# A gated state-space convolution on one core: seeds written to PSUM by ScalarE, a second table stored slot by slot, and the log step as one row

## The chip, the cores and the metric

The kernel runs on one core of a Trainium2 chip. The metric is the device time in microseconds (us); the median of three runs of the kernel before is 164.76 us (164.47 to 164.81). Engines are named as the profile names them: PE (matmuls; PEld is its weight load), DVE (VectorE), ACT (ScalarE), POOL (GpSimd), SP (the queue that issues most DMAs). Each engine takes its instructions strictly in the order of its own list, and engines wait for each other by semaphores.

## The reference

`x` is 2048 tokens of 512 channels in bf16. The output is `g*a + (1-g)*b`. `g` is a sigmoid of a dot product per token. `b` is `x`, with a small gated network added at the two tokens that rank highest. `a` is a state-space convolution:

```python
dt = jnp.exp(log_dt)[:, None]
logdA = dt * A                       # A complex, 512 channels x 128 states
dB = dt * Bc
P = jnp.exp(logdA[:, :, None] * l)   # l = 0..2047
K = jnp.einsum("dn,dnl,dn->dl", Cc, P, dB).real
# y = causal convolution of u with K along the tokens, by FFT, plus u * Dskip
```

## The kernel before, in words

**Two halves.** The 512 channels are worked in two halves `h` of 256, the 2048 tokens in two blocks `blk` of 1024.

**Tables.** A power `exp(logdA * l)` is split into a product of two tables, because a lag `l` is written as a sum of a coarse and a fine lag. `tab1(h)` makes table 1 (`TP[h]`), with 32 coarse lags. `tab2(h)` makes table 2: the magnitudes `EB` come from ACT's Exp (`exps2`), the angles pass through `trig` (a scaling into int32, `L455`; a Sin on ACT; a quarter-turn addition, `L611`; a second Sin), and DVE multiplies them (helper `TT`, `L436`). From 11 magnitudes and angles DVE builds the four weighted tables `r[0]` to `r[3]` with 21, 17, 21 and 17 slots. In memory a group of 4 channels keeps all its slots together, so the innermost run of an operand is 4 elements times the slots. The weights `WW` are `C * B * dt`, made at the start by `PBR`, `CM1`, `CM2`, `CMW` and a last multiply by `DTB = exp(log_dt)`; `log_dt` is loaded as a 128-fold broadcast.

**Kernel spectrum.** `kgen(h)` multiplies table 1 with table 2 on PE (`L819`, 256 matmuls of 84 or 68 columns per half) and ACT copies the sums to `KA`. Three small sets of matmuls (`L832`, `L836`, `L845`, `L848`) pick the entries into `KC`. `kspec(h)` turns `KC` into the spectrum `KK[h]` for two segments `i` (`L865`). For `i = 1` the sum carries over the other part of segment 0 with alternating sign, by two 512-column matmuls with a diagonal of plus and minus one (`kc`, `L872`). Each of the 16 pieces of `KK` over both halves is copied from PSUM by ACT (`L451`).

**Input spectrum, products and inverse.** `forward(blk)` (`L801`) makes the input's spectrum `X`. `products(h)` is DVE alone (`L436`): per half eight multiplies or adds of 4096 elements and some sixteen of 1024 elements. `inverse(h)` accumulates in PSUM, for 16 token blocks per half: `fin` starts a bank with `DG * U` (`L919`: the input, scaled by a diagonal that holds `(1-g)/g` per token) and `OHR * ZB` (`L920`: rows for single tokens), then the inverse transform is added (`L933`), and a copy scaled by `g` writes the result (`L941`), which a DMA stores.

**What sets the order.** The program lists 627 operations. `ORDER` is a string of their numbers, three characters each, that fixes the order on every engine. Many copies and scalings have two forms, one for ACT and one for DVE: the string `SECOND` chooses, one digit per operation (helpers `EV`, `SCL` and the quarter-turn addition). `PLACES` gives each temporary its PSUM bank (eight of them) or buffer place; an operation that takes a place waits for all uses of the holder before. No engine can pass over an operation that waits.

Of the kernel before, what the change touches and what calls it, by code (L numbers as in the profile page):

```python
# [337 lines left out]
def small_mats():  # L338
    eye = np.eye(128)
    sgn = np.diag(np.where(np.arange(128) % 2 == 0, 1.0, -1.0))  # L340
# [17 lines left out]
    "02z04j06305n04v04k04l01n01e03603704m06403803003903103a01304105103b01l02503201202401r03c03d05a05902703u02200b03e04w03g03h05q05205r03f02a03i01802301t04n"
    "04z02003j05o03k06601p05s03l04203m05c03n02900m05002b01y03o03p04o03q05t02802605306504x03r06705b04y05w03s05u05d05605405505p05705x05e05g05y07d05803z06l07f"
    "04005f07e07g06x05h07h06z07i04804506y03v03w05z05v07005i07j04307107807607507707906007207306807a07b08y08x03t06m09603x08z04604407404909907c06103y01404a07l"  # L360
    "08w07n09709807k09004706g09a06f07m07p07o06a07z07s04b04c07y06907q07v07w04d04e07t09106h06i06n09207u06p09b07r07x06o08008209s06s09r08109t09309406b09q06j06k"
# [659 lines left out]
```

## Time and profile before

| what | value |
|---|---|
| median of three runs | 164.76 us |
| profiled execution, its own time | 164.17 us |
| its span in the trace | 162.3 us, so 1.87 us lie around the span |
| PE busy | 141.7 us, 87% of the span |
| DVE busy | 151.5 us, 93% |
| ACT busy | 120.0 us, 74% |
| granted TensorE clock, mean | 0.989 |
| DMA moved | 18.00 MB |

How to read it: busy time counts an instruction from its start to its end. Two instructions that follow each other on one engine without a wait overlap a little, so what one more instruction costs is read from start to start. Most DVE work has one helper line, `L436`, so its shapes have to be kept apart.

### The profile page before, as it was taken

What the parts mean: (1) busy time and instruction counts of PE and PEld (TensorE: products, weight loads), DVE (VectorE), ACT (ScalarE), POOL (GpSimd) and SP (SyncE); (2) the same over time, 40 slices, a digit from 0 to 9 for tenths busy, and PEclk for the clock granted to TensorE, in tenths of its full rate; (3) what the DMA queues carried; (4) which work ended last, traced back from release to release, by engine and by line L of the source; (5) the groups of instructions that cost most, each with busy time, mean ns of one, the idle gap of its engine ahead of it and who ended that gap; (6) DMA issues with size and microseconds to landing.
All of it is one profiled execution on the core that took longest, in us unless ns stands there. A gap on an engine that the chain in (4) does not pass through costs nothing.

```text
span 162.3 us, 3993 instructions
## 1 busy us (share of the span) xinstructions
PE 141.7 (87%) x1721; PEld 104.7 (65%) x1733; DVE 151.5 (93%) x234; ACT 120.0 (74%) x181; POOL 4.1 (3%) x10
## 2 busy tenths in 40 slices
PE   0579996869999999999777997999999999999990
PEld 0456642335763634686675867977888888788880
DVE  0499999999999999999999999999999999999982
ACT  3399999999999999999999595756783522260461
POOL 3000020000000000000000000040000000000000
PEclk9999999999999999999987999999999999999999
DMA  2999999900000000000790000007700020023036
GB/s 73 334 398 367 413 406 383 312 13 0 4 0 0 4 0 0 4 0 4 220 408 22 4 2 0 4 4 222 307 0 0 0 69 0 2 66 99 0 106 185
DMA packets 11251, 18.00 MB, mean 111 GB/s; under 512 B 857, under 2 KB 7898, under 8 KB 11106
## 3 DMA queue, kind: packets, MB, share of 16 engines
q1 hardware_dynamic: 10114, 16.97, 29.5%
q10 hardware_dynamic: 1120, 0.79, 1.7%
q8 instruction: 13, 0.21, 0.5%
q14 instruction: 4, 0.03, 0.1%
HBM read 15.66 MB, written 2.10 MB: 109 GB/s over the span
## 4 chain that ended last, share of the span: by engine, by line
DVE 48%; PE 10%; ACT 0%; issue 0%
DVE AR L436 43%; PE ps L933 9%; DVE AR L455 2%; DVE AR L611 1%; DVE AR L941 1%; PE ps L920 1%; PE ps L919 1%; ACT AR L941 0%; DVE AR L445 0%
## 5 line engine op out<-in xcount | busy, mean ns | idle before, releaser
L436 DVE TENSOR_TENSOR AR<-AR 128x1024 bf16<-128x1024 bf16 (+8 forms) x121 | 114.1, 997 | 0.4
L451 ACT ACTIVATE AR<-ps 128x1024 bf16<-128x1024 f32 (+5 forms) x48 | 42.6, 930 | 14.1 <-PE ps L865 4.0
L447 ACT ACTIVATE AR<-AR 128x512 bf16<-128x512 f32 (+4 forms) x73 | 50.5, 753 | 2.8 <-DVE AR L436 1.8
L801 PE MATMUL ps<-AR 128*128 128x512 bf16 x183 | 41.8, 379 | 1.4 <-DVE AR L445 0.4
L801 PEld LDWEIGHTS ps<-AR 128*128 128x128 bf16 x192 | 18.0, 98 | 21.0 <-DVE AR L445 0.9
L933 PE MATMUL ps<-AR 128*128 128x256 bf16 x256 | 30.6, 273 | 0.2 <-DVE AR L436 0.2
L933 PEld LDWEIGHTS ps<-AR 128*128 128x128 bf16 x256 | 24.8, 98 | 4.1 <-DVE AR L436 1.0
L941 ACT ACTIVATE AR<-ps,AR 128x256 bf16<-128x256 f32 x27 | 11.9, 473 | 19.3 <-PE ps L933 19.0
L819 PEld LDWEIGHTS ps<-AR 128*128 128x128 bf16 x512 | 18.1, 97 | 3.3 <-ACT AR L451 2.0
L819 PE MATMUL ps<-AR 128*128 128x84 bf16 (+1 forms) x512 | 18.6, 197 | 1.5 <-DVE AR L436 0.9
L865 PE MATMUL ps<-AR 128*128 128x256 bf16 x160 | 19.0, 275 | 0.9 <-ACT AR L451 0.9
L865 PEld LDWEIGHTS ps<-AR 128*128 128x128 bf16 x160 | 15.3, 99 | 4.6 <-ACT AR L451 2.0
L455 DVE TENSOR_SCALAR AR<-AR 128x256 int32<-128x256 f32 (+2 forms) x41 | 12.6, 328 | 0.1
L455 ACT ACTIVATE AR<-AR 128x256 int32<-128x256 f32 (+1 forms) x25 | 11.2, 482 | 0.0
L557 PE MATMUL ps<-AR 128*128 128x128 bf16 x24 | 3.1, 308 | 5.7 <-DMA AR<-c_bf 5.7
L920 PE MATMUL ps<-AR 128*128 128x256 bf16 x32 | 7.8, 273 | 0.0
L919 PE MATMUL ps<-AR 128*128 128x256 bf16 x32 | 7.8, 272 | 0.0
L611 DVE TENSOR_SCALAR AR<-AR 128x1024 int32<-128x1024 int32 x10 | 6.9, 687 | 0.1
L436 DVE TENSOR_TENSOR AR<-AR,ps 128x512 f32<-128x512 bf16 x1 | 0.7, 689 | 6.5 <-PE ps L557 6.5
L557 PEld LDWEIGHTS ps<-AR 128*128 128x128 bf16 x24 | 2.3, 139 | 6.0 <-DMA AR<-c_bf 5.7
L670 PE MATMUL ps<-AR 128*128 128x128 bf16 x64 | 4.7, 222 | 1.1 <-DMA AR<-in_A_u_dram 0.7
L832 PE MATMUL ps<-AR 128*32 128x128 bf16 x64 | 5.0, 422 | 0.4 <-ACT AR L451 0.4
(57 smaller groups left out, 88.3 us busy)
## 6 DMA issues: line engine op xcount, KB each, us to landing
AR<-c_ksp SPq DMA_DIRECT2D x5, 512.0 KB, 5.6
AR<-in_A_u_dram SPq DMA_DIRECT2D x4, 512.0 KB, 6.2
AR<-c_fwd SPq DMA_DIRECT2D x4, 512.0 KB, 12.1
AR<-c_inv SPq DMA_DIRECT2D x1, 2048.0 KB, 7.8
AR<-in_B_w_up_dram SPq DMA_DIRECT2D x1, 1792.0 KB, 14.7
AR<-in_B_w_gate_dram SPq DMA_DIRECT2D x1, 1792.0 KB, 18.2
out_dram<-AR SPq DMA_DIRECT2D x14, 128.0 KB, 2.2
AR<-in_B_w_down_dram SPq DMA_DIRECT2D x1, 1024.0 KB, 13.7
```

Of the source, the lines that this page charges most:

```text
L436: return P.op(DVE, lambda h: h.tensor_tensor(out=o, in0=a, in1=b, op=op), rd, wr, cost=tt_cost(o, a, b), **k)
L447: return P.op(ACT, lambda h: h.activation(out=o, in_=a, func=func, scale=scale, bias=bias), rd, wr, cost=0.185 + nel(o) * 0.833e-3 + (0.09 ...
L451: return P.op((ACT, DVE), (lambda h: h.activation(out=o, in_=a, func=ACTF.Copy), lambda h: h.tensor_copy(o, a)), rd, wr, cost=(0.185 + n * ...
L455: return P.op((ACT, DVE), (lambda h: h.activation(out=o, in_=a, func=ACTF.Copy, scale=c), lambda h: h.tensor_scalar(out=o, in0=a, scalar1= ...
L611: P.op((DVE, ACT), (lambda hh: hh.tensor_scalar(out=w, in0=w, scalar1=16384.0, scalar2=None, op0=ALU.add), lambda hh: hh.activation(out=w, ...
L801: last = h.matmul(o, w, x, start=(pm + par + st == 0), stop=(par == 1 and st == 3), skip_group_check=(pm == 1))
L819: last = hh.matmul(pb(0, 128, g // 6 * 512 + g % 6 * W4 + o, (1, n)), TP[h][1 - i // 2](0, 128, (b0 + g) * 128, (1, 128)), r[i](0, 128, (b ...
L865: last = hh.matmul(pb(0, 128, n * 256, (1, 256)), KP[u](0, 128, tau * 128, (1, 128)), KC[h](0, 128, jg * 256, (1, 256)), start=(k == 0 and ...
L919: hh.matmul(pb(0, 128, e * 256, (1, 256)), DG(0, 128, tb[e] * 128, (1, 128)), U(0, 128, tb[e] * D + h * HC, (1, HC)), start=(e == 0), stop ...
L920: last = hh.matmul(pb(0, 128, e * 256, (1, 256)), OHR(0, 128, tb[e] * 128, (1, 128)), ZB(0, 128, h * HC, (1, HC)), start=False, stop=False)
L933: r = hh.matmul(pb(0, 128, e * 256, (1, 256)), G(0, 128, ((par * 2 + part) * 4 + ft) * 512 + (2 * t2 + e) * 128, (1, 128)), X(0, 128, h * ...
L941: P.op((ACT, DVE), (lambda hh, o=o, i_=i_, g_=g_: hh.activation(out=o, in_=i_, func=ACTF.Copy, scale=g_), lambda hh, o=o, i_=i_, g_=g_: hh ...
```

## The change

**Seeds.** In `kspec`, for `i = 1`, ACT copies the carry from `KK` straight into the PSUM banks, scaled by a sign per partition (`SGN`, a new 1 KB load), and the matmuls add to it; the 16 matmuls `kc` go. In `inverse`, ACT writes `U * (1-g)/g` into each half bank (32 copies of 256 elements) and only the `OHR * ZB` matmul of `fin` remains; the 32 matmuls on `DG`, `DG` itself (one DVE multiply of 2048 elements) and its small copy in `SGB` go. A seeded bank has to follow a holder that matmuls wrote in full.

**Table 2.** `EB`, `DI`, `QA`, `NB` and `r` are stored slot by slot: 256 channels of a slot lie together. Multiplies that differ only in an operand's offset become one instruction. `kgen` now reads its columns from `r` in runs of 4 elements, 512 bytes apart.

**Log step and weights.** `log_dt` is loaded as one row of 1 KB; a matmul with a row of ones spreads it over the partitions in PSUM, and Exp reads it there. `dt` is multiplied into `B` (`BDT`, in place of the copy `PBR`), so that the last multiply into `WW` goes.

**Order.** `ORDER`, `SECOND` and `PLACES` are replaced whole (644 operations). At the start SP now issues the row, the identity (`c_bf`) and `A_im`, ACT issues `A_re`. The copy `XE` may run on either engine. Costs noted for the ordering (`STT`) change without effect on the program.

```diff
-    sgn = np.diag(np.where(np.arange(128) % 2 == 0, 1.0, -1.0))
...
-    return np.concatenate([eye, sgn, -sgn, xs.reshape(128, -1), ek.reshape(128, -1)], 1), oh
...
-        DQ([(LDT(0, 128, 0, (1, D)), dr(A_log_dt, 0, (0, 128), (1, D)))], [], [LDT], 131072, eng=ACT)
-        prm_l(0)
         DQ([(CB(0, 128, 0, (1, 128)), cb_c[:, 0:128])], [], [(CB, "i")], 32768)
-        prm_l(1, eng=ACT)
+        prm_l(0, eng=ACT)
+        DQ([(LDT(0, 1, 0, (1, D)), dr(A_log_dt, 0, (D, 1), (1, D)))], [], [LDT], 1024)
+        prm_l(1)
+        P.op(POOL, lambda h: h.memset(ONE(0, 1, 0, (1, 128)), 1.0), [], [ONE], cost=0.2)
...
+        DQ([(SGN(0, 128, 0, (1, 2)), sg_c[:, :])], [], [SGN], 1024)
...
-        AC(f512(DTB), f512(LDT), ACTF.Exp, [LDT], [DTB], tset=0)
+        ld = misc()
+        P.op(PE, lambda h: h.matmul(ld(0, 128, 0, (1, D)), ONE(0, 1, 0, (1, 128)), LDT(0, 1, 0, (1, D)), start=True, stop=True), [LDT, ONE], [ld], cost=0.22)
+        AC(f512(DTB), ld(0, 128, 0, (1, D)), ACTF.Exp, [ld], [DTB], tset=0)
...
-        P.op((ACT, DVE), (lambda h: h.activation(out=w4(PBR, 0, (D, 2)), in_=pp(3, 0, (D, 2)), func=ACTF.Copy), lambda h: h.tensor_copy(w4(PBR, 0, (D, 2)), pp(3, 0, (D, 2)))), [pps[3]], [PBR], cost=(1.04, 1.23))
-        TT(w4(CM1, 0, (D, 2)), pp(2, 0, (D, 2)), w4(PBR, 0, (0, 2)), ALU.mult, [pps[2].buf, PBR], [CM1])
-        TT(w4(CM2, 0, (D, 2)), pp(2, 0, (D, 2)), w4(PBR, D, (0, 2)), ALU.mult, [pps[2].buf, PBR], [CM2])
-        TT(f512(CMW), f512(CM1), f512(CM2, D), ALU.subtract, [CM1, CM2], [(CMW, 0)])
-        TT(f512(CMW, D), f512(CM1, D), f512(CM2), ALU.add, [CM1, CM2], [(CMW, 1)])
-        TT(c2(WW), c2(CMW), DTB(0, 128, 0, (0, 2), (1, D)), ALU.mult, [CMW, DTB], [WW])
+        TT(w4(BDT, 0, (D, 2)), pp(3, 0, (D, 2)), w4(DTB, 0, (0, 2)), ALU.mult, [pps[3], DTB], [BDT])
+        TT(w4(CM1, 0, (D, 2)), pp(2, 0, (D, 2)), w4(BDT, 0, (0, 2)), ALU.mult, [pps[2], BDT], [CM1])
+        TT(w4(CM2, 0, (D, 2)), pp(2, 0, (D, 2)), w4(BDT, D, (0, 2)), ALU.mult, [pps[2], BDT], [CM2])
+        TT(f512(WW), f512(CM1), f512(CM2, D), ALU.subtract, [CM1, CM2], [(WW, 0)])
+        TT(f512(WW, D), f512(CM1, D), f512(CM2), ALU.add, [CM1, CM2], [(WW, 1)])
...
-                    AC(two(EB[0], EB[1], i * 4, 4 * NM), AL(0, 128, 0, (HC, 2), (4, 64), (1, 4)), ACTF.Exp, [AL], [(EB[0], ("e", i)), (EB[1], ("e", i))], scale=float(m), tset=ts)
...
+                    AC(pair(EB[0](0, 128, i * HC, (1, HC)), EB[1](0, 128, i * HC, (1, HC))), AL(0, 128, 0, (HC, 2), (1, HC)), ACTF.Exp, [AL], [(EB[0], ("e", i)), (EB[1], ("e", i))], scale=float(m), tset=ts)
...
-                return s(0, 128, k * n, (4, na_), (4 * na_, 64), (1, 4))
+                return s(0, 128, k * n, (4, na_), (4 * na_, 64), (1, 4)) if wide else s(0, 128, k * n, (HC, na_), (4, 64), (1, 4))
...
-                v = lambda b: b(0, 128, 4 * a0, (EW_, 64), (1, 4 * na_))
-                sv = lambda k: s(0, 128, k * na_ * HC, (4 * na_, 64), (1, 4 * na_))
-                if h == 0:
-                    TT(pair(v(di), v(eb)), pair(v(eb), v(eb)), pair(sv(0), sv(2)), MUL, [(s, "s"), (s, "c")], ek + [(di, g)])
-                else:
-                    TT(v(di), v(eb), sv(0), MUL, ek + [(s, "s")], [(di, g)])
-                    TT(v(eb), v(eb), sv(2), MUL, [(s, "c")], ek)
+                v = lambda b: b(0, 128, a0 * HC, (1, na_ * HC))
+                sv = lambda k: s(0, 128, k * na_ * HC, (1, na_ * HC))
+                TT(pair(v(di), v(eb)), pair(v(eb), v(eb)), pair(sv(0), sv(2)), MUL, [(s, "s"), (s, "c")], ek + [(di, g)])
...
-            TT(q(0), ww(1), bo(di), MUL, [WW] + dk, [(qa, 0)])
-            TT(q(1), ww(1), bo(eb), MUL, [WW] + ebk, [(qa, 1)])
-            TT(w(0), ww(0), bo(eb), MUL, [WW] + ebk, [(r[0], "w")])
-            TT(w(2), ww(0), bo(di), MUL, [WW] + dk, [(r[2], "w")])
+            sl = lambda b, j, *d: b(0, 128, j * HC, *d, (1, HC))
+            ww = lambda p: WW(0, 128, p * D + h * HC, (0, NOF), (1, HC))
+            bo = lambda b: sl(b, NST, (HC, NOF))
+            q = lambda i: sl(qa, i * NOF, (HC, NOF))
+            w = lambda i: sl(r[i], 0, (HC, NOF))
+            TT(pair(q(0), q(1)), pair(ww(1), ww(1)), pair(bo(di), bo(eb)), MUL, [(WW, 1)] + dk + ebk, [(qa, 0), (qa, 1)])
+            TT(pair(w(0), w(2)), pair(ww(0), ww(0)), pair(bo(eb), bo(di)), MUL, [(WW, 0)] + ebk + dk, [(r[0], "w"), (r[2], "w")])
...
-                for k, (j, a0, n) in enumerate(RAWS):
-                    o = o0 + sum(x[2] for x in RAWS[:k])
-                    bw = 4 * NJ if b is not nb else 4 * NOF
-                    TT(r[i](0, 128, 4 * o, (4 * (NJ, NR)[i % 2], 64), (4, n), (1, 4)), a(0, 128, 4 * a0, (EW_, 64), (4, n), (1, 4)), b(0, 128, 4 * j, (bw, 64), (0, n), (1, 4)), MUL,
-                       (ebk if a is eb else dk) + [(b, ka)], [(r[i], k)])
+                (j, a0, n), (j1, _, _), (j2, a2, n2) = RAWS
+                ak = (ebk if a is eb else dk) + [(b, ka)]
+                TT(sl(r[i], o0, (n * HC, 2), (HC, n)), sl(a, a0, (0, 2), (HC, n)), sl(b, j, ((j1 - j) * HC, 2), (0, n)), MUL, ak, [(r[i], 0)])
+                TT(sl(r[i], o0 + 2 * n, (HC, n2)), sl(a, a2, (HC, n2)), sl(b, j2, (0, n2)), MUL, ak, [(r[i], 2)])
...
-            CP(SGB(0, 128, 64, (2, 16), (1, 2)), SG(0, 128, 96, (1, 16), (0, 2)), [(SG, "x")], [(SGB, "x")])
...
-            CP(XE(32, NE, 0, (1, D)), xe(32, NE, 0, (1, D)), [xe.buf], [XE])
+            EV(XE(32, NE, 0, (1, D)), xe(32, NE, 0, (1, D)), [xe.buf], [XE])
...
-            TT(DG(0, 128, 0, (128, 16), (2, 64), (1, 2)), IDN(0, (0, 16), (2, 64), (1, 2)), SGB(0, 128, 64, (2, 16), (0, 64), (1, 2)), MUL, [CBI, (SGB, "x")], [DG])
...
                                 last = hh.matmul(pb(0, 128, g // 6 * 512 + g % 6 * W4 + o, (1, n)), TP[h][1 - i // 2](0, 128, (b0 + g) * 128, (1, 128)),
-                                                 r[i](0, 128, (b0 + g) * n, (1, n)), start=(i == 0), stop=(i == 3))
+                                                 r[i](0, 128, (b0 + g) * 4, (HC, n // 4), (1, 4)), start=(i == 0), stop=(i == 3))
...
-                        pb = psum(2)
+                        pb = psum(2, full=True, seed=i == 1)
                         taus = [part * 8 + pm * 4 + 2 * qd + e for pm in range(2) for e in range(2)]
+                        if i:
+                            AC(pb(0, 128, 0, (1, 1024)), KK[h](0, 128, (1 - part) * 2048 + qd * 1024, (1, 1024)), ACTF.Copy, [SGN, (KK[h], (0, 1 - part, qd))], [pb], scale=SGN(0, 128, part, (1, 1)))
                         def ks(hh, taus=taus, uses=uses, pb=pb, i=i, part=part):
                             last = None
                             for n, tau in enumerate(taus):
                                 for k, u in enumerate(uses):
                                     jg = KUSE[u][1]
-                                    last = hh.matmul(pb(0, 128, n * 256, (1, 256)), KP[u](0, 128, tau * 128, (1, 128)), KC[h](0, 128, jg * 256, (1, 256)), start=(k == 0 and (i == 0 or n % 2 == 0)), stop=(k == len(uses) - 1 and i == 0))
+                                    last = hh.matmul(pb(0, 128, n * 256, (1, 256)), KP[u](0, 128, tau * 128, (1, 128)), KC[h](0, 128, jg * 256, (1, 256)), start=(k == 0 and i == 0 and n % 2 == 0), stop=(k == len(uses) - 1 and n % 2 == 1), skip_group_check=(i == 1))
                             return last
                         P.op(PE, ks, [KP[u] for u in uses] + [(KC[h], KUSE[u][1]) for u in uses], [pb.buf], cost=4 * len(uses) * 0.1095)
-                        if i:
-                            def kc(hh, pb=pb, part=part, qd=qd):
-                                last = None
-                                for pm in range(2):
-                                    last = hh.matmul(pb(0, 128, pm * 512, (1, 512)), CB(0, 128, 256 if part == 0 else 128, (1, 128)),
-                                                     KK[h](0, 128, (1 - part) * 2048 + qd * 1024 + pm * 512, (1, 512)), start=False, stop=True)
-                                return last
-                            P.op(PE, kc, [(CB, "o"), (KK[h], (0, 1 - part, qd))], [pb.buf], cost=2 * 0.2157)
...
-                        pb = bufs[t2, par] = misc()
+                        pb = bufs[t2, par] = psum(seed=True)
+                        for e, tb in enumerate(tbs(t2, par)):
+                            AC(pb(0, 128, e * 256, (1, 256)), U(0, 128, tb * D + h * HC, (1, HC)), ACTF.Copy, [(SG, "x"), (U, (tb, h))], [(pb, e)], scale=SG(0, 128, 96 + tb, (1, 1)))
                         def fin(hh, pb=pb, tb=tbs(t2, par)):
                             last = None
                             for e in range(2):
-                                hh.matmul(pb(0, 128, e * 256, (1, 256)), DG(0, 128, tb[e] * 128, (1, 128)), U(0, 128, tb[e] * D + h * HC, (1, HC)), start=(e == 0), stop=False)
-                                last = hh.matmul(pb(0, 128, e * 256, (1, 256)), OHR(0, 128, tb[e] * 128, (1, 128)), ZB(0, 128, h * HC, (1, HC)), start=False, stop=False)
+                                last = hh.matmul(pb(0, 128, e * 256, (1, 256)), OHR(0, 128, tb[e] * 128, (1, 128)), ZB(0, 128, h * HC, (1, HC)), start=False, stop=False, skip_group_check=True)
                             return last
-                        P.op(PE, fin, [DG, OHR, (ZB, "y"), (ZB, ("e", h)), (ZB, "d")] + [(U, (t, h)) for t in tbs(t2, par)], [pb.buf], cost=4 * 0.1092)
+                        P.op(PE, fin, [OHR, (ZB, "y"), (ZB, ("e", h)), (ZB, "d")], [pb], cost=2 * 0.1092)
```

More of the change, by code (lines that the diff above doesn't have):

```diff
@@ L55, with __init__ @@
 class Life:
-    def __init__(self, prog, pool, n, home, region, name):
+    def __init__(self, prog, pool, n, home, region, name, full=False, seed=False):
+        self.full, self.seed = full or seed, seed
         self.prog, self.pool, self.n, self.region, self.name = prog, pool, n, region, name
@@ L150, in fixed @@
             ls.sort(key=lambda l: min(at[i] for i in l.all))
+            assert not ls[0].seed
             for a, b in zip(ls, ls[1:]):
+                assert a.full or not b.seed, "a seeded bank follows one that was not written in full"
                 assert max(at[i] for i in a.all) < min(at[i] for i in b.all), "a place is held twice"
@@ L358 @@
[L358 to L361, printed above, removed]
@@ L390, in bass_gated_mix__ssm_conv_s4__moe_arch_mod__prompt_kernel @@
     oh_c = const(oh, "c_oh")
+    sg_c = nc.inline_tensor(np.stack([np.where(np.arange(128) % 2 == 0, -1.0, 1.0), np.where(np.arange(128) % 2 == 0, 1.0, -1.0)], 1).astype(np.float32), "c_sgn").ap()
     cf = np.zeros((128, 160), np.float32)
@@ L418, in bass_gated_mix__ssm_conv_s4__moe_arch_mod__prompt_kernel, with psum @@
         oEND = 190 * KB + NM * 512
-        def psum(n=1, dt=F32, name="ps"):
+        def psum(n=1, dt=F32, name="ps", full=False, seed=False):
             def home(u):
@@ L422, in home @@
                 return (a if dt == F32 else a.bitcast(dt)), (u % 2) * (2048 // (4 if dt == F32 else 2))
-            return Life(P, "ps", n, home, None, name)
+            return Life(P, "ps", n, home, None, name, full, seed)
         def npe(n):
@@ L442, in STT @@
         def STT(o, a, sc, b, op0, op1, rd, wr, **k):
-            return P.op(DVE, lambda h: h.scalar_tensor_tensor(out=o, in0=a, scalar=sc, in1=b, op0=op0, op1=op1), rd, wr, cost=0.16 + nel(o) * 1.25e-3, **k)
+            return P.op(DVE, lambda h: h.scalar_tensor_tensor(out=o, in0=a, scalar=sc, in1=b, op0=op0, op1=op1), rd, wr, cost=0.16 + nel(o) * 1.02e-3, **k)
         def CP(o, a, rd, wr, **k):
@@ L790, in forward @@
                 for ft in range(4):
-                    pb = psum(2)
+                    pb = psum(2, full=True)
                     for pm in range(2):
@@ L826, in kgen @@
             for bk in range(2):
-                pb = misc()
+                pb = psum(full=True)
                 def sel(hh, bk=bk, pb=pb):
```

64 lines of the change are left out of this document (31 added, 33 removed).

## The prediction

> **What bounds the kernel now.** I read first the page's forty slices, then busy time by stretches cut where the work changes, then the chain of waits.
>
> ```profile
> PE   0579996869999999999777997999999999999990
> DVE  0499999999999999999999999999999999999982
> ACT  3399999999999999999999595756783522260461
> ```
>
> ```profile
> 60.00:90.00 30.00, 26.43 (x397) 19.25 (x397) 29.97 (x50) 29.41 (x41) 0.00 (x0) 0.94 0.25 89
> 90.00:98.42 8.42, 7.71 (x62) 5.68 (x60) 8.42 (x12) 6.77 (x8) 0.00 (x0) 1.00 0.01 3
> 98.42:116.55 18.13, 17.55 (x365) 15.67 (x366) 17.94 (x15) 10.85 (x14) 1.81 (x1) 1.00 0.33 117
> 116.55:140.14 23.59, 23.25 (x203) 19.66 (x204) 23.59 (x24) 10.97 (x17) 0.00 (x0) 1.00 0.05 14
> 140.14:156.43 16.29, 16.29 (x148) 14.35 (x149) 16.05 (x17) 5.73 (x13) 0.00 (x0) 1.00 0.18 52
> 156.43:162.30 5.87, 1.96 (x18) 1.51 (x16) 2.24 (x5) 1.75 (x4) 0.00 (x0) 1.00 0.61 171
> ```
>
> The columns are the stretch, its length, then busy time of PE, PEld, DVE, ACT and POOL, clock and DMA. DVE is full from its first instruction to the last product at 156.43. ACT is full with it until about 90 and then only about half busy; PE is nearly full from 98.42 on. 5.87 us follow the last product.
>
> ```profile
> 66.78 0.20 DVE AR L455
> 66.98 1.14 DVE AR L436
> 68.12 0.34 DVE AR L455
> 71.13 0.60 DVE AR L611
> 80.19 0.60 DVE AR L436
> 116.55 23.55 DVE AR L436 x23
> 141.19 0.11 PE ps L919
> 147.74 6.99 PE ps L933 x64
> ```
>
> This is the chain, its pieces from start to start. It ends on PE because the last inverse matmuls run there, but DVE's products run beside it to 156.43: two engines end together. So the end moves only if DVE, PE and ACT all allow it, and DVE sets the least. The piece at 66.98 has 2048 elements and that at 80.19 has 1024; hence 0.54 us per 1024 elements and 0.06 us per instruction. Whole DVE durations below are longer by the overlap of about 0.08.
>
> **The start.**
>
> ```profile
> 1.57 0.43 SPq L458 DMA_DIRECT2D AR<-c_bf  x1
> 4.73 0.63 ACT L447 ACTIVATE AR<-AR 128x512 bf16<-128x512 bf16 x1 [0.84 <-DMA AR<-in_A_log_dt_dram]
> 5.74 0.77 PEld L557 LDWEIGHTS ps<-AR 128*128 128x128 bf16 x8 [5.74 <-DMA AR<-c_bf]
> 6.47 0.69 DVE L436 TENSOR_TENSOR AR<-AR,ps 128x512 f32<-128x512 bf16 x1 [6.47 <-PE ps L557]
> ```
>
> DVE's first instruction waits for transposes, and these for the identity, issued third on SP and landed 4.17 after its issue. In the new order it goes second, one issue (0.41) earlier: -0.4. The log row, first on SP, would land by about 4.9 even with the identity's delay; a matmul and the Exp (0.63) come after, 5.9 in all, just ahead of the transposes at 6.06. Late next is then the second row for `W8`, now issued behind three 512 KB loads of `U`; its copy `WL` has DVE's 5.6 us of earlier work as cover (by the chain's prices). `SGN` (1 KB) has the whole first stage. Ends: -0.8 if the broadcast also slowed the loads beside it, +0.5 if row or `W8` come late. I take -0.4.
>
> **DVE up to its first product** (98.42 before).
>
> ```profile
> L436 DVE TENSOR_TENSOR AR<-AR 128x2048 bf16<-128x2048 bf16 x19 | 22.9, 1214 | 0.0
> L436 DVE TENSOR_TENSOR AR<-AR 128x1024 bf16<-128x1024 f32 x1 | 1.2, 1219 | 0.0
> L573 DVE COPY AR<-ps 128x1024 bf16<-128x1024 bf16 x1 | 1.2, 1215 | 0.0
> L445 DVE CAST AR<-ps 8x512 bf16<-8x512 f32 x1 | 0.7, 683 | 0.0
> ```
>
> - The last multiply into `WW` goes: 1.219 less the overlap, -1.14. `BDT` replaces the copy `PBR` element for element: 0.
> - `XE` moves to ACT by the new digits: -0.60. The small `SGB` copy: -0.1.
> - Table 2: in half 1 three pairs of multiplies merge, in each half four products with `WW` become two and twelve products become eight. 3+4+8 = 15 instructions at 0.06: -0.9; the elements stay. Longer runs can hardly be slower than today's runs of 4 elements, which already go at 0.54 per 1024.
> - The digits of `SECOND`, compared operation by operation: 15 scalings of 256 (0.20 each) leave DVE and 11 come; two additions of 1024 (0.60) leave and two of 768 come (about 0.47); one negation (0.34) and one copy of 336 from PSUM (about 0.45) come; pairs of 1024-copies and of final copies swap evenly. -0.3.
>
> Sum -3.0, so with the start DVE is ready at 95.0.
>
> **ACT up to the same point.** Here the change adds a wait. In the new order the product on `KK` of segment 1 comes first, so DVE needs both seeded pieces.
>
> ```profile
> 90.71 1.02 ACT L451 ACTIVATE AR<-ps 128x1024 bf16<-128x1024 f32 x1 [1.25 <-PE ps L865]
> 92.46 3.77 ACT L451 ACTIVATE AR<-ps 128x1024 bf16<-128x1024 f32 x4 [0.72 <-PE ps L865]
> 96.45 2.85 ACT L451 ACTIVATE AR<-ps 128x1024 bf16<-128x1024 f32 x3 [0.22 <-PE ps L872]
> 143.41 2.22 ACT L941 ACTIVATE AR<-ps,AR 128x256 bf16<-128x256 f32 x5 [0.40 <-PE ps L933]
> L447 ACT ACTIVATE AR<-AR 128x1024 bf16<-128x1024 int16 x24 | 24.6, 1050 | 0.2
> ```
>
> Start to start an ACT copy of 1024 costs (3.77-1.02)/3 = 0.92, one of 256 with a scale per partition (2.22-0.47)/4 = 0.44. No row shows ACT writing PSUM: the seed of 1024 is bounded by 0.92 and by 1.05, whole, from SBUF; I take 0.95. Before, eight copies of `KK[0]` ended at 99.30. Now four lie behind the first product (-3.7), two seeds come before it (+1.9), and `SECOND` adds four scalings (about 0.3 each), widens two additions and takes away a negation and a copy: +0.4. Of the 2.2 us that ACT waited here for PE, some 0.5 should stay, since a quarter-turn and a Sin of table 1 now fill it: -1.7. With the start: 99.3-0.4-1.4-1.7 = 95.8. So DVE waits 0.8 for a seeded piece, with every later product queued behind; if ACT is quicker the wait is 0.
>
> [...]
>
> **From the first product to the end.** DVE: the `DG` multiply of 2048 goes (1.214 less overlap), -1.14; the rest stays: 95.8 + 58.01 - 1.14 = 152.7, and 5.87 after it.
>
> PE must not take over. Removed here: 32 `fin` matmuls at 0.109 (the 0.11 above) and eight of 512 at twice that, -5.2, hidden today behind DVE. If that cover were gone, they would be worth 5.2. Added: half of `kspec(0)`, 2.6, and slower columns of `kgen`:
>
> ```profile
> 98.64 8.95 PE L819 MATMUL ps<-AR 128*128 128x84 bf16 x256 [0.88 <-DVE AR L436]
> 109.43 0.30 PE L836 MATMUL ps<-AR 128*32 128x64 bf16 x2
> 111.02 1.16 PE L848 MATMUL ps<-AR 128*32 128x64 bf16 x8
> L836 PE MATMUL ps<-AR x4: 242/244/248, 109.4 to 109.6; 128*32 128x64 bf16 x4
> L848 PE MATMUL ps<-AR x8: 302/305/306, 111.0 to 111.9; 128*32 128x64 bf16 x8
> ```
>
> `kgen` costs (8.95-0.20)/255 = 34 ns per matmul of 76 columns on average. `L848` reads single elements 168 bytes apart: (1.16-0.305)/7 = 122 ns for 64 columns, 1.9 ns per run. `L836` reads them 8 bytes apart, 0.06 us for 64, 0.97 ns per column. Both also write with gaps. If 1.9 ns is the price of a new stretch of 16 bytes (two of `L836`'s elements share one), a run of 4 costs 0.48 ns per column: 37 ns, up to 39 with an instruction's own part, +0.6 to +1.3 per half. If the price is `L836`'s per column, 74 ns. I take the first, as it fits both rows.
>
> [...]
>
> PE: 17.55+23.25+16.29+1.96 = 59.1, less 5.2, plus 2.6 and 0.6 to 1.3: 57.1 to 57.8 from 95.0, thus 152.1 to 152.8, against DVE's 152.7 and 1.96 of matmuls after it, 154.7. Some 2 us of room for waits.
>
> ACT: 29.3 busy there before; plus four `KK` copies 3.7, `XE` 0.5, six seeds 5.7 and 32 of 256 (bounds 0.31, as a scaling, and 0.47, the whole final copy; taken 0.44) 14.1: 53.3 in 58.8.
>
> **The sum.** -0.4 -3.0 +0.8 -1.14 = -3.8 (rounded): span 158.5, own time 164.17 - 3.8 = 160.4. The median shown lies 0.6 above the profiled execution; from it 164.76 - 3.8 = 161.0.
>
> **Rivals.**
>
> *A: larger gain.* No wait for the seeded piece, and the early loads land sooner too: -5.3, 159.5. For it, the seeds' low bound; against it, ACT is as full as DVE up to 90. 0.10.
>
> *B: ACT holds the end back.* A seed stands in ACT's list ahead of copies and can start only when its bank is free; until then the copies behind it and the matmuls that need those banks wait. Speaking for it:
>
> ```profile
> ACT AR L941 <- PE ps L933: 19.0, 9, 6.5
> ```
>
> ACT waited 19.0 us for inverse matmuls; now it has 5.5 us spare. Each us of waits beyond these goes to the end. At 8 it is +2.3: 163.2. Against it: the seeds stand early in the new order, well ahead of their matmuls. 0.20.
>
> *C: the columns of `kgen` decide, slower.* At `L836`'s 0.97 ns per column each matmul costs 74 ns, 40 more, 10.1 us per half. In half 1 PE has about 2 us of room: +8; in half 0 PE idles 3.6 us between 60 and 90, so up to 6 more can reach ACT's copies. 161.0 + 8 and more: 170. It outweighs the gain from +23 ns per matmul ((3.8+2)/256). For it: both rows are slow. Against it: their common price per 16 bytes. 0.09.
>
> *D: nothing.* ACT's second pieces come 3 us later than summed, and DVE waits off its saving at 95. For it: the chain copy, seed, matmul, copy is longer than before. 164.7. 0.06.
>
> **How the numbers follow.** Forecast 0.55, A 0.10, B 0.20, C 0.09, D 0.06. The prediction is 161.0. The range: A's 159.5 with a little below, and B with the early loads' +0.5 above, 159.3 to 163.8; C, most of D and the tails stay out. Faster by over 0.2% (which a measurement of this kernel can just tell) 0.85, within it 0.06, slower 0.09.
>
> **What would show it.** DVE's first instruction near 6.1; its first product near 95.8, with a wait on ACT under 1 us; `L819` at 37 to 39 ns per matmul; `L872` gone, `L919` gone; from first product to last 56.9 on DVE without idle; ACT above 85% busy after 100; the span near 158.5. The forecast is wrong if DVE idles over 1.5 us after its first product, if that product starts after 97, or if PE runs without a gap to the end and DVE's last product waits.

## The result and the profile after

The changed kernel took 160.62 us (median of 4 runs, 159.72 to 161.2) against 164.78 for the kernel before (164.47 to 164.84): a ratio of 0.975, with a 95% interval of 0.969 to 0.980. The forecast was 161.0. The profiled execution took 159.72, with a span of 157.9 in place of 162.3.

From the page of the changed kernel, the forty slices:

```profile
PE   3599889999799999999137999998997999999990
DVE  0699999999999999999999999999999999999982
ACT  4799899999999999999999999997899999939531
PEclk9999999999999999999956999999999999999999
```

ACT is now full almost to the end, where it was half busy from 90 us on. The new hole is on PE, in slices 20 and 21, and PE's clock is low just behind its start, in slices 21 and 22.

Busy time in stretches cut at DVE's first instruction, its first product and the end of its last product (length, PE, PEld, DVE, ACT, POOL, clock, DMA); the kernel before had 91.95, 58.01 and 5.87 us:

```profile
4.13:95.22 91.09, 79.03 (x962) 51.49 (x972) 88.81 (x156) 89.14 (x134) 0.47 (x1) 0.96 0.39 143
95.22:151.95 56.73, 54.42 (x694) 46.58 (x693) 56.35 (x53) 48.45 (x85) 1.81 (x1) 1.00 0.17 58
151.95:157.90 5.95, 2.17 (x20) 1.70 (x18) 2.33 (x5) 1.79 (x4) 0.00 (x0) 0.95 0.60 173
```

The first product comes 3.20 us earlier than before (95.22 against 98.42), the stretch of the products is 1.28 shorter, the rest 0.08 longer: 4.40 together, the difference of the spans.

The start, in the timeline:

```profile
0.73 0.32 SPq L461 DMA_DIRECT2D AR<-in_A_log_dt_dram  x1
2.02 0.60 PE L567 MATMUL ps<-AR 1*128 1x512 bf16 x1 [2.02 <-DMA AR<-in_A_log_dt_dram]
3.25 0.59 PE L561 MATMUL ps<-AR 128*128 128x128 bf16 x4 [0.63 <-DMA AR<-c_bf]
3.42 0.60 ACT L450 ACTIVATE AR<-ps 128x512 bf16<-128x512 f32 x1
4.13 0.69 DVE L439 TENSOR_TENSOR AR<-AR,ps 128x512 f32<-128x512 bf16 x1 [4.13 <-ACT AR L450]
5.21 1.46 PE L561 MATMUL ps<-AR 128*128 128x128 bf16 x12 [1.36 <-DMA AR<-in_A_A_im_dram]
5.85 0.69 DVE L446 SCALAR_TENSOR_TENSOR AR<-ps,AR 128x512 f32<-128x512 bf16 x1 [1.04 <-PE ps L561]
```

DVE starts 2.34 us earlier than before, then stands 1.04 for `A_im`. With the usual overlap of 0.08 lost there, the start gained about 1.2, not 0.4. Two loads came sooner than forecast: the log row was there at 2.02, and the transposes that wait for the identity (`c_bf`) began at 3.25, where the identity came at 5.74 in the kernel before.

The seeds and the first products (ACT, then DVE; the row at 93.78 is the second of the five copies from 92.67 on):

```profile
89.52 1.12 ACT L450 ACTIVATE ps<-AR 128x1024 f32<-128x1024 bf16 x1
90.56 1.02 ACT L454 ACTIVATE AR<-ps 128x1024 bf16<-128x1024 f32 x1
91.62 1.12 ACT L450 ACTIVATE ps<-AR 128x1024 f32<-128x1024 bf16 x1
92.67 4.65 ACT L454 ACTIVATE AR<-ps 128x1024 bf16<-128x1024 f32 x5
93.78 1.02 ACT L454 ACTIVATE AR<-ps 128x1024 bf16<-128x1024 f32 x1
77.60 22.11 DVE L439 TENSOR_TENSOR AR<-AR 128x2048 bf16<-128x2048 bf16 x18
```

DVE runs through from 77.60 to 99.7: the first product, at 95.22, waited for nothing. It needs the two seeded pieces, which are the first two copies from 92.67 on; the second ended at 94.80, only 0.4 us before DVE came to the product. A seed of 1024 takes 1.04 from start to start.

### The profile page after: what moved, and what is told of

Its sections match the earlier page's. It is cut to its first block, busy times and chain, and to the rows that moved or that the text cites. A ratio compares the mean times of both kernels' runs of the same rounds, so it can differ in the third digit from the quotient of the medians.

```text
span 157.9 us, 3936 instructions
## 1 busy us (share of the span) xinstructions
PE 136.8 (87%) x1677; PEld 100.2 (63%) x1686; DVE 147.5 (93%) x213; ACT 141.3 (89%) x224; POOL 3.9 (2%) x11
## 4 chain that ended last, share of the span: by engine, by line
DVE 67%; ACT 12%; PE 11%; issue 5%; DMA 2%; SPq 0%
DVE AR L439 56%; PE ps L924 10%; ACT AR L450 10%; DVE AR L458 4%; DVE AR L454 3%; DMA AR<-in_A_A_im_dram 2%; DVE AR L616 2%; ACT L220 2%; PE ps L911 1%; DVE AR L446 0%; SPq L461 0%; PE ps L561 0%; DVE AR L448 0%; DVE AR L932 0%; DVE AR L444 0%
## 5 line engine op out<-in xcount | busy, mean ns | idle before, releaser
L439 DVE TENSOR_TENSOR AR<-AR 128x1024 bf16<-128x1024 bf16 (+9 forms) x104 | 110.5, 1114 | 0.7 <-ACT AR L450 0.2
L450 ACT ACTIVATE AR<-AR 128x512 bf16<-128x512 f32 (+2 forms) x72 | 49.5, 755 | 1.7 <-DVE AR L439 1.0
L454 ACT ACTIVATE AR<-ps 128x1024 bf16<-128x1024 f32 (+6 forms) x48 | 43.3, 931 | 2.0 <-POOL AR L772 0.7
L797 PEld LDWEIGHTS ps<-AR 128*128 128x128 bf16 x192 | 18.1, 98 | 21.8 <-ACT AR L454 1.4
L924 PE MATMUL ps<-AR 128*128 128x256 bf16 x256 | 30.1, 273 | 0.2 <-DVE AR L439 0.2
L924 PEld LDWEIGHTS ps<-AR 128*128 128x128 bf16 x256 | 24.7, 98 | 3.9 <-DVE AR L439 0.9
L450 ACT ACTIVATE ps<-AR 128x256 f32<-128x256 bf16 (+1 forms) x40 | 23.0, 609 | 0.3
L863 PE MATMUL ps<-AR 128*128 128x256 bf16 x160 | 19.3, 273 | 1.4 <-ACT ps L450 1.1
L815 PEld LDWEIGHTS ps<-AR 128*128 128x128 bf16 x512 | 18.1, 97 | 1.4 <-ACT AR L454 0.6
L863 PEld LDWEIGHTS ps<-AR 128*128 128x128 bf16 x160 | 14.9, 98 | 5.1 <-ACT ps L450 2.1
L616 DVE TENSOR_SCALAR AR<-AR 128x1024 int32<-128x1024 int32 (+1 forms) x10 | 6.6, 660 | 0.2 <-ACT AR L450 0.2
L911 PE MATMUL ps<-AR 128*128 128x256 bf16 x32 | 5.6, 273 | 0.1
L454 DVE CAST AR<-ps 128x1024 bf16<-128x1024 f32 (+1 forms) x5 | 5.4, 1073 | 0.0
L561 PE MATMUL ps<-AR 128*128 128x128 bf16 x24 | 3.1, 310 | 2.6 <-DMA AR<-in_A_A_im_dram 1.4
L454 DVE COPY AR<-ps 128x1024 bf16<-128x1024 bf16 x8 | 5.2, 678 | 0.0
```

Of the source, the lines that this page charges most:

```text
L439: return P.op(DVE, lambda h: h.tensor_tensor(out=o, in0=a, in1=b, op=op), rd, wr, cost=tt_cost(o, a, b), **k)
L450: return P.op(ACT, lambda h: h.activation(out=o, in_=a, func=func, scale=scale, bias=bias), rd, wr, cost=0.185 + nel(o) * 0.833e-3 + (0.09 ...
L454: return P.op((ACT, DVE), (lambda h: h.activation(out=o, in_=a, func=ACTF.Copy), lambda h: h.tensor_copy(o, a)), rd, wr, cost=(0.185 + n * ...
L616: P.op((DVE, ACT), (lambda hh: hh.tensor_scalar(out=w, in0=w, scalar1=16384.0, scalar2=None, op0=ALU.add), lambda hh: hh.activation(out=w, ...
L797: last = h.matmul(o, w, x, start=(pm + par + st == 0), stop=(par == 1 and st == 3), skip_group_check=(pm == 1))
L815: last = hh.matmul(pb(0, 128, g // 6 * 512 + g % 6 * W4 + o, (1, n)), TP[h][1 - i // 2](0, 128, (b0 + g) * 128, (1, 128)), r[i](0, 128, (b ...
```

## The experiments

Once its loads are in, the kernel repeats itself closely. Two landmarks on DVE cut each trace: the first addition into `WW` (17.39 us in the trace above) and the first product. In two traces of the changed kernel the stretch between them is 77.83 and 77.82 us long, and from the first product to the end of the last both have 56.73. Single executions are read by these stretches.

### The changed kernel again

> The changed kernel once more, unaltered, beside the kernel before. The single times so far lie from 159.7 to 161.2 us, five times as wide as those of the kernel before. If the trace of 159.72 us shows the usual execution, the median stays at 160.6 and the spread comes from the start (when the loads of the parameters land); if it was a lucky one, the median comes out near 161.0.

161.37 us (160.48 to 162.36) against 164.07 (163.99 to 164.51); ratio 0.983, 0.980 to 0.986. So the change is worth some 2.7 to 4.2 us, and its executions lie about four times as far apart as those of the kernel before. In this trace `WW` came 0.87 later than in the first one, and all that follows kept this distance. Its waits of DVE (total us, how often, the longest):

```profile
DVE AR L439 <- PE ps L561: 0.9, 1, 0.9
DVE AR L454 <- PE ps L668: 0.5, 1, 0.5
```

`L561` transposes `C_re` here, `L668` the first tiles of `U`. One source of the spread is how fast the first loads land. A second one was found below.

### One DVE multiply more, late and early

```diff
+ TT(half(o2(p)), half(x2(1)), half(k2(0)), MUL, ...)      # ahead of the first product of half 0
```
```diff
+ TT(pair(w(0), w(2)), pair(ww(0), ww(0)), pair(bo(eb), bo(di)), MUL, ...)   # table 2, half 1
```

> One multiply of 2048 elements more on DVE right at the first product of half 0 (its result is overwritten with the same values). Theory 1, DVE sets the end from its first product to its last: +1.14 us over the changed kernel. Theory 2, ACT sets it (seeds and copies fill 92 to 98% of 95 to 135 us): 0 to +0.4.

> One multiply of 2048 elements more on DVE in table 2 of half 1, near 74 us (overwritten with the same values). Theory 1, DVE sets the pace up to its first product: +1.14 us over the changed kernel. Theory 2, ACT (99% busy from 30 to 90 us) sets the pace there and DVE follows it: 0 to +0.5.

162.1 us (ratio 0.987, 0.985 to 0.990) and 162.36 (0.989, 0.985 to 0.992): by the ratios +0.7 and +0.9 over the repeated run, with the intervals overlapping. The stretches say it more sharply. Products with the late multiply; then, for the early one, from the first product of table 2 in half 0 to that in half 1, with the late kernel's same stretch ahead of it, since both have the same dip of PE's clock before (0.50 from 48 to 52 us):

```profile
97.69:155.57 57.88, 54.62 (x694) 46.67 (x693) 57.50 (x54) 48.52 (x85) 1.81 (x1) 1.00 0.17 57
```
```profile
48.32:82.20 33.88, 29.85 (x345) 17.72 (x346) 32.39 (x45) 32.19 (x49) 0.00 (x0) 0.94 0.08 27
```
```profile
49.78:84.76 34.98, 29.70 (x345) 17.73 (x346) 33.52 (x45) 33.22 (x49) 0.00 (x0) 0.94 0.12 38
```

+1.15 over 56.73, and +1.10: in both places DVE's added work comes out in full.

### One ACT copy more, early

```diff
+ for p in range(2):
+     AC(f512(SCR), f512(WW, p * D), ACTF.Copy, ...)
```

> Two copies of 512 elements more on ACT (1.04 us together) near 58 us, into a buffer that nobody reads. Theory 1, DVE sets the pace and ACT runs ahead of it: 77.8 us from the first addition into WW to the first product grows by 0 to 0.3. Theory 2, ACT, 99% busy from 30 to 90 us, is as late as DVE: +0.9 to +1.0.

One execution, 162.61 us. A wait of 1.4 at 20 us, ahead of the added copies, lengthened the stretch named in the expectation, so it is read from the first table-2 product of half 0 to the first product instead; the changed kernel, then this one:

```profile
47.47:95.22 47.75, 40.60 (x477) 26.73 (x478) 47.47 (x58) 47.18 (x66) 0.00 (x0) 0.93 0.15 56
```
```profile
49.70:98.11 48.41, 40.71 (x479) 26.58 (x478) 47.68 (x58) 48.02 (x68) 0.00 (x0) 0.93 0.15 55
```

+0.66 of 1.04: neither theory. DVE now stands in short waits for ACT between 75 and 81 us. ACT is some 0.4 us ahead of DVE and no more; up to the first product both engines bind.

### The small seeds undone

```diff
- AC(pb(...e * 256...), U(...), ACTF.Copy, scale=SG(...96 + tb...))
+ hh.matmul(pb(...e * 256...), DG(...), U(...), start=(e == 0), stop=False)
+ TT(DG(...), IDN(...), SGB(...), MUL, ...)
```

> The 32 seeds of 256 columns go back to 32 matmuls with a diagonal, and with them come back the multiply of 2048 on DVE and the small copy that build the diagonal. Theory 1, DVE sets the end: from DVE's first product to the end of its last one 56.7 becomes 57.9 (+1.14), although ACT loses 13 us of work and PE gains 3.5. Theory 2, ACT holds the end back (it is 98% busy from 112 to 135): the stretch becomes shorter than 56.7, down to 55.5. Theory 3, PE has no room for 3.5 more: longer than 58.5, or more than 5.9 us behind the last product.

One execution, 164.11 us:

```profile
97.37:155.11 57.74, 56.16 (x716) 49.08 (x714) 57.40 (x54) 36.61 (x53) 1.81 (x1) 1.00 0.17 55
155.11:162.30 7.19, 3.40 (x32) 2.81 (x29) 2.33 (x5) 1.79 (x4) 0.00 (x0) 0.92 0.57 162
```

ACT lost 12 us and the stretch became no shorter: ACT does not hold the end. DVE's multiply brought +1.01, and PE is 1.24 us later behind the last product (7.19 against 5.95). The 3.5 us that PE lost by the change were not all hidden: 1.2 of them count.

### The carry seeds undone

```diff
- AC(pb(...), KK[h](...), ACTF.Copy, scale=SGN(...))
+ hh.matmul(pb(... pm * 512 ...), CB(sign diagonal), KK[h](...), start=False, stop=True)   # pm = 0, 1
```

> The eight seeds of 1024 columns go back to sixteen matmuls of 512 with a sign diagonal, behind their group's matmuls. ACT loses 8.3 us, PE gains 3.5. Theory 1, the seeds of the carry spectrum are worth nothing by themselves, because the first product did not wait for a seeded piece: both stretches of DVE stay, 77.8 us from the first addition into WW to the first product, 56.7 from there to the end of the last one. Theory 2, the copies on ACT set when the products can run: the second stretch gets shorter by 0.5 or more.

One execution, 161.94 us:

```profile
18.65:96.95 78.30, 69.58 (x872) 43.87 (x873) 76.71 (x134) 74.31 (x111) 0.47 (x1) 0.98 0.27 97
96.95:154.17 57.22, 56.49 (x708) 48.42 (x707) 56.42 (x52) 42.85 (x79) 1.81 (x1) 1.00 0.18 58
```
```profile
DVE AR L440 <- ACT AR L455: 0.8, 2, 0.5
```

Both theories fell. DVE waits twice for an ACT copy, 0.48 more in the first stretch and 0.49 in the second: the products need the pieces of `KK` sooner than PE delivers them with the matmuls of 512 ahead of the copies. The carry seeds bring about 1.0 us.

### The merged multiplies split

```diff
- TT(pair(q(0), q(1)), pair(ww(1), ww(1)), pair(bo(di), bo(eb)), MUL, ...)
+ TT(q(0), ww(1), bo(di), MUL, ...)
+ TT(q(1), ww(1), bo(eb), MUL, ...)      # and so for the other merged ones: 15 more
```

> The merged multiplies of table 2 are split again, 15 instructions more on DVE with the same elements. Theory 1: 0.06 us each, +0.9 in the stretch from the first addition into WW to the first product (77.8 in the changed kernel, without clock dips of PE), all of it at the end too. Theory 2, ACT sets the pace up to 90 us: 0 to +0.4.

One execution, 162.56 us. The first stretch is 79.72, +1.89. Of that, 0.66 is a wait for PE that comes from a dip of its clock (0.58 from 44 to 48 us) and 0.12 a longer wait for a Sin:

```profile
DVE AR L449 <- PE ps L767: 0.6, 1, 0.6
```

The 15 instructions keep 1.11, 0.07 each: from start to start a merged multiply of 3584 elements takes 1.94 and its two parts 1.00 each.

### The order of the first loads

```diff
- SP: log row, identity, A_im, B_re, U, C_re, U, ...    ACT: A_re, C_im, B_im
+ SP: identity, A_im, log row, B_re, C_re, U, U, ...    ACT: A_re, B_im, C_im
```

> Only the order of five loads is changed: A_im ahead of the log row on SP, C_re ahead of the first 512 KB of U, B_im ahead of C_im on ACT. Theory 1, the gain of the changed kernel varies from execution to execution because DVE, which now starts at 4.13 us, then waits for A_im and C_re (1.1 us in the trace of 157.9, 2.0 in the one of 158.8, 3.2 in the one of 162.9): these waits go below 0.8, the median falls by 0.8 to 1.5 us below that of the unaltered changed kernel (161.4 on the chip of its last run) and the executions at the usual clock lie closer together. Theory 2, ACT, which is as full as DVE up to 90 us, takes up what DVE gains at the start: DVE waits as much later on, and the median stays.

161.37 us against 164.12; ratio 0.979, 0.976 to 0.983: not told apart from the unaltered kernel. The waits moved:

```profile
1.61 0.33 SPq L461 DMA_DIRECT2D AR<-in_A_log_dt_dram  x1
3.89 0.60 PE L567 MATMUL ps<-AR 1*128 1x512 bf16 x1 [3.89 <-DMA AR<-in_A_log_dt_dram]
5.24 0.69 DVE L439 TENSOR_TENSOR AR<-AR,ps 128x512 f32<-128x512 bf16 x1 [5.24 <-ACT AR L450]
11.15 0.69 DVE L454 COPY AR<-ps 128x1024 bf16<-128x1024 bf16 x1 [0.90 <-PE ps L668]
```

The log row, no longer first, came for a matmul at 3.89 in place of 2.02, so DVE started 1.1 later, and `U` came later than DVE's copy of it. `A_im` and `C_re` held nothing up. Theory 1 named the right waits, but what was taken from them came back elsewhere: this order shifts the wait from one load to another.

### The log step spread by its load

```diff
- h.matmul(ld(...), ONE(0, 1, ...), LDT(0, 1, ...)); AC(f512(DTB), ld(...), ACTF.Exp)
+ DQ([(LDT(0, 128, ...), dr(A_log_dt, 0, (0, 128), (1, D)))], eng=ACT)   # first; A_im second on ACT; A_re first on SP
+ AC(f512(DTB), f512(LDT), ACTF.Exp)
```

> The log step is again spread over the partitions by its load (128 KB, first on ACT), without the matmul; A_re goes first on SP, the identity stays second. Theory 1, with the start paced by how fast the loads land, the row by a matmul is worth little: DVE's first instruction moves from 4.1 to about 5.4, but it waits less for A_im and C_re, and the first addition into WW starts within 0.5 us of the 17.4 to 18.6 seen so far. Theory 2, the row brings what the first instruction shows: that addition starts 1.0 to 1.3 us later, near 19.3.

162.41 us against 164.12; ratio 0.988, 0.985 to 0.991.

```profile
6.08 0.69 DVE L439 TENSOR_TENSOR AR<-AR,ps 128x512 f32<-128x512 bf16 x1 [6.08 <-PE ps L561]
19.65:98.27 78.62, 70.69 (x870) 43.98 (x871) 76.54 (x134) 76.96 (x113) 0.47 (x1) 0.96 0.25 91
```

Theory 2: the addition into `WW` starts at 19.65, where the other traces, but for one with 19.6, have 17.4 to 18.7. The row by a matmul is worth 1.0 us against the unaltered kernel's median (162.41 - 161.37), and about 2 against the kernel with the fillers below (160.35), which like this one shows no dip of PE's clock near 44 us (1.00 from 40 to 60 us in both). In this trace some 0.8 comes on top behind that landmark: the stretch in the row is that much longer than 77.83, with a wait of DVE for PE of 1.3 us that ends at 25 us, while PE's clock was 0.50 from 22 to 24 us. And 6.08 is what the forecast had for the identity alone (6.47 less 0.4).

The times from issue to landing show what the row changed besides the Exp, first in the changed kernel, then here:

```profile
AR<-in_A_A_re_dram ACTq DMA_DIRECT2D x1, 128.0 KB, 2.2
AR<-c_bf SPq DMA_DIRECT2D x1, 32.0 KB, 2.0
```
```profile
AR<-in_A_A_re_dram SPq DMA_DIRECT2D x1, 128.0 KB, 3.4
AR<-c_bf SPq DMA_DIRECT2D x1, 32.0 KB, 4.2
```

With the 128-fold load the identity takes 4.2 us, as it did before the change (4.1), and `A_re` 3.4, although it now goes out first on SP. So the loads beside the 128-fold load landed 1.2 to 2.2 us later. Two things were not taken apart: whether its 128 reads of one row do this or its 128 KB, and what the identity loses by standing behind 128 KB of `A_re` in its queue.

### Filler matmuls on PE

```diff
  for fb in range(14): ...          # second group of 56 matmuls of 2 columns
+     for _ in range({6: 2, 13: 3}.get(fb, 0)):
+         h.matmul(bb(0, 128, 64, (1, 448)), W(0, 0), U(0, 128, 0, (1, 448)), start=True, stop=True)
```

> Five matmuls of 448 columns, whose result nobody reads, are put into the second group of 56 matmuls of 2 columns of the expert layer (near 42 us), where PE streams next to nothing for 1.5 us and then waits 1.25 us for ACT. In two executions traced at a mean clock of 0.967, PE's clock was 0.56 to 0.87 from 42 to 54 us, and DVE then waited 1.6 us more between 69 and 80 us than in those at 0.989; about a third of the executions of the changed kernel have that clock, none of the kernel before. Theory 1, the near-empty stretch lets the clock fall: no execution below 0.975, the slowest ones go, the median falls by 0.3 to 0.6 us. Theory 2, the clock falls for another reason: a third of the executions still show 0.968.

The matmuls near 42 us in the kernel with the late multiply, its PE and clock behind them (the number before the last two is the clock), and the same stretches with the fillers:

```profile
41.60 1.54 PE L746 MATMUL ps<-AR 128*128 128x2 bf16 x56
44.39 2.21 PE L797 MATMUL ps<-AR 128*128 128x512 bf16 x7 [1.25 <-ACT AR L454]
```
```profile
44.00:48.00 4.00, 3.61 (x63) 2.51 (x66) 4.00 (x10) 3.97 (x7) 0.00 (x0) 0.67 0.01 4
48.00:52.00 4.00, 3.76 (x15) 1.29 (x14) 4.00 (x8) 4.00 (x8) 0.00 (x0) 0.50 0.00 0
```
```profile
44.00:48.00 4.00, 4.00 (x69) 2.45 (x68) 4.00 (x12) 3.97 (x7) 0.00 (x0) 1.00 0.02 4
48.00:52.00 4.00, 4.00 (x22) 1.68 (x21) 4.00 (x8) 4.00 (x8) 0.00 (x0) 1.00 0.00 0
```

160.35 us (159.58 to 160.69) against 164.12; ratio 0.976, 0.973 to 0.979, on the chip on which the unaltered kernel had 0.983 (0.980 to 0.986). No execution has a mean clock below 0.976, where two of the six of the unaltered kernel had 0.968 and took 162.0 and 162.4. This version beats both kernels, and Theory 1 is the one that fits. It rests on few executions: with the four of the first measurement, two in ten of the unaltered kernel had the low clock, and none in five here or in five of the next kernel, which has the fillers too (0.973 and above).

### A seed earlier

```diff
- ACT: copy (0,0,qd 1), copy (1,0,qd 0), seed       DVE: ..., h1 product, h0 product, ...
+ ACT: copy (0,0,qd 1), seed, copy (1,0,qd 0)       DVE: ..., h0 product, h1 product, ...
```

> On top of the five filler matmuls, one seed of 1024 (the one for which PE waited 0.92 us at 120.8) goes ahead of one copy on ACT, and one product of half 0 ahead of a product of half 1 on DVE, so that DVE does not wait for the later copy. Theory 1, PE runs about 1.2 us behind DVE at the end (eleven inverse matmuls lie ahead of the last product's on PE when it ends), so the time that PE no longer waits is gained: DVE's stretch from its first product to the end of its last one stays 56.7, and what follows it falls from 6.0 to about 5.1 us; the median falls by 0.7 to 0.9 below the 160.35 of the kernel with the fillers alone. Theory 2, DVE alone sets the end: 6.0 stays, no change. Theory 3, the copy that now comes later holds up a product: the stretch grows by up to 1.0.

160.74 us against 164.2; ratio 0.979, 0.977 to 0.981: no gain.

```profile
96.23:152.97 56.74, 54.73 (x695) 46.49 (x693) 56.36 (x53) 48.60 (x85) 1.81 (x1) 1.00 0.18 58
152.97:158.90 5.93, 2.17 (x20) 1.70 (x18) 2.33 (x5) 1.79 (x4) 0.00 (x0) 1.00 0.60 174
```
```profile
PE ps L865 <- ACT ps L450: 0.5, 2, 0.3
PE ps L913 <- ACT ps L450: 0.5, 2, 0.3
```

PE's wait of 0.92 went and shorter ones for other seeds came; the stretch behind the last product stayed. With the fillers alone PE waits 0.20 for a product of DVE at 137.5 and runs without a gap from there to the end. So what it gains ahead of that point is lost there, and only less work behind it would shorten the end; that was not tried.

### Columns of other layouts

```diff
- r[i](0, 128, (b0 + g) * 4, (HC, n // 4), (1, 4))                       # both halves
+ r[i](0, 128, b0 + g, (64, n))  or  r[i](..., (128, n // 2), (1, 2))     # half 1, by table
```

> The columns that PE streams are laid out differently, so the values are wrong in half 1 and in the selection of half 0, and only prices are read. In the second kgen, its tables of 84 columns are read as single elements 128 bytes apart and those of 68 as pairs 256 bytes apart, in place of runs of 4 elements 512 bytes apart, which cost no more than columns without a gap (34.8 ns per matmul against 34.7 before). In the selection of half 0 the first group writes its columns without a gap and still reads single elements 168 bytes apart, the second reads without a gap and still writes 16 bytes apart. Theory 1 (a new 16-byte stretch costs 1.9 ns, unless two columns share it): single elements 1.9 ns per column, 160 ns per matmul of 84; pairs 0.5 to 1.0, 34 to 65 ns per matmul of 68; the first group stays at 1.9 ns per column and the second falls to 0.42. Theory 2 (the gapped output sets the price): single elements 0.42 ns per column, 35 ns; the first group falls to 0.42 to 0.5, the second stays.

The changed kernel's second `kgen` and this one's, then its selection:

```profile
95.49 3.46 PE L815 MATMUL ps<-AR 128*128 128x84 bf16 x96
```
```profile
96.20 10.04 PE L815 MATMUL ps<-AR 128*128 128x84 bf16 x96
82.08 2.00 PE L830 MATMUL ps<-AR 128*32 128x128 bf16 x32 [5.93 <-ACT AR L454]
```

34 ns per matmul against 104. By the starts of the single matmuls the single elements cost 145 ns per 84 columns (1.73 ns each) and the pairs 62 ns per 68 (0.91 per column, 1.8 per pair), at a clock of 1.00 (96 to 100 us) and of 0.50 (101 to 106) alike. The selection's four tiles of 32 run side by side (in the changed kernel's trace the four matmuls of a step start within 0.01 us of each other, and the steps 0.24 apart), so a step of four matmuls is one pass of 128 columns: 0.213 us with the output closed up (1.66 ns per column), 0.241 with the input closed up (1.88). Theory 1 for the input; but in this selection the gapped output alone costs as much, and neither theory had both. PE's clock was 0.50 here; with both gaps a step took 0.24 at a clock of 1.00 too, in the kernel before.

## Why the prediction was right, step by step

**The sum** held: 4.4 us in the traces against 3.8, and 2.7 to 4.2 in the medians. That it came so close is in part luck, since its parts did not all hold. The start gave 0.8 more than forecast, DVE's work 0.5 more, and the wait of 0.8 did not come. Against these 2.1 us stand 1.6 of idle time on DVE that the sum had at nothing.

- **The start (-0.4) was mis-sized.** The step that failed is the time of two loads: the log row "would land by about 4.9", and the identity was given its old 4.17 us after issue. They were there at 2.02 and 3.25. Had the identity taken 4.17 again, DVE could not have started before 6.1, as the run with the 128-fold load shows (6.08); the earlier issue alone gives 0.4. Taking that load away brought 1 to 2 more: the sum named this as its end of -0.8 and did not use it. `A_im`, which the forecast did not follow, took 1.1 of it back, and up to 1.7 in a later trace.
- **DVE's work (-3.0)** came out at -3.5. Summed over the single instructions, without waits and without the extra time of one that needs the result just ahead of it, 90.9 us before are 87.4 after. The merges came out at 0.07 each in place of 0.06, the multiplies are confirmed by the two runs with one more (1.1 each). What the forecast lacked is that this work no longer runs without gaps. Besides the wait for `A_im` DVE stands 1.6 us more than before: 1.2 in four short waits, three of which are in the rows below, and the rest in more places where an instruction needs the one just ahead of it (0.12 each).

```profile
DVE AR L458 <- ACT AR L450: 0.2, 1, 0.2
DVE AR L616 <- ACT AR L450: 0.2, 1, 0.2
DVE AR L697 <- PE ps L702: 0.2, 1, 0.2
```

- **The wait of 0.8 for a seeded piece** did not come, because ACT was sooner: the pieces were ready at 94.80, not 95.8, while DVE came at 95.22, close to the forecast's 95.0. ACT shares the gain of the start, and of the 0.5 us that it was to wait for PE some 0.1 is left, just ahead of the copy at 93.78. The price of the seed was wrong the other way: 1.04 from start to start, not 0.95. The smaller seeds cost 0.40, not 0.44.
- **The products (-1.14)** held: 56.73 against the forecast 56.87.
- **PE's 5.2 us "hidden today behind DVE"** was half right. With 3.5 of them back, PE is 1.2 later at the end; the forecast's 2 us of room would have left 1.5. The other matmuls taken off PE were worth 1.0, through the copies that DVE waits for.
- **`kgen` (37 to 39 ns)** was a little too dear: 34 ns, as before. A piece of input cost 1.7 to 1.8 ns in the run with other layouts, where the next lay 128 bytes away or more, and four columns without a gap took PE as long (34 ns for 76 columns in the kernel before, 1.8 for four). That a piece is 16 bytes long was the author's estimate from two rows of before; where between 8 and 128 bytes a new one begins was not shown. Rival C is out.
- **Rival B** is out: ACT waits 6.6 us for inverse matmuls, not 19.0, and is 85% busy behind the first product, but a kernel with 12 us less on ACT there ends no sooner. What the forecast names but gives no price is ACT ahead of the first product, where it is only 0.4 us ahead of DVE. Rival B's own time was mis-added: 8 us of waits less 5.5 spare is +2.5, so 163.5, not +2.3 and 163.2.
- **Rival A** had the mechanism of the first trace, with a chance of only 0.10: no wait for the seeded piece, and early loads that land sooner. Its -5.3 became -4.4 because `A_im` and the short waits took some of it back.

The prices of the parts taken out one by one (2.3 for the small seeds, 1.0 for the carry seeds, 1.1 for the merges, 1 to 2 for the row, and 1.1 for the multiply into `WW`, the last by adding one like it) add up to 6.5 to 7.5, more than the whole gain. The undone kernels keep an order of work that was made without those parts; how much of the excess this explains was not measured.

## What to carry to other kernels

Cut the trace at landmarks of the engine that sets the pace: stretches repeated to 0.01 us here, while medians moved by 1 us. Follow every load of a start that is brought forward, not only the one that was last, since the next one takes the gain back (`A_im` 1.1 us of it here). A matmul taken away is free only as far as PE keeps ahead at the end and in the chain to the copies that others wait for (putting them back cost 1.2 and 1.0 us here).
